# New cost tables and offsets for the planner of a fused attention and gated-MLP kernel

## The chip, the cores and the metric

The kernel runs on one core of one Trainium2 chip. The metric is the device time of one execution in microseconds; a kernel's time is the median over its runs. The engines are TensorE (PE, with its weight loads PEld), VectorE (DVE), ScalarE (ACT), GpSimd (POOL) and SyncE (SP). SP issues all of the kernel's DMAs, on one queue.

## The reference

Four batches of 768 tokens, eight heads of 64 channels. Each query sees the keys less than 16 positions away, and 24 block keys, each the channel-wise maximum over 32 keys; the block values are means over 32 values. One softmax runs over both kinds. The result goes through a gated MLP (512 to 1536 to 512). The MLP's weights come as float64.

```python
k_sum = k.reshape(B, H, nb, block, D).max(axis=3)
v_sum = v.reshape(B, H, nb, block, D).mean(axis=3)
mask_l = np.abs(pos[:, None] - pos[None, :]) < window
scores_s = scale * np.einsum('bhsd,bhnd->bhsn', q, k_sum) + np.log(block)
scores_all = np.concatenate([np.where(mask_l, scores_l, -1e9), scores_s], axis=-1)
a = softmax(scores_all)          # exp, sum + 1e-9, division
x = np.matmul(a, np.concatenate([v, v_sum], axis=2))    # then heads side by side
g = x @ w_gate
out = (g * (1.0 / (1.0 + np.exp(-g))) * (x @ w_val)) @ w_out
```

## The kernel before

**Attention** works on units `(k, u)`: `k` is one of eight half batches of 384 tokens, `u` one of four pairs of heads. For a unit, TensorE makes the scores of six tiles of 64 queries against 96 keys and 24 block keys (step `SC`, line 561). DVE finds the maxima (`max`, or `ttr` from the second batch on), ACT does six `exp` steps with running sums, and `eps`, `rcp` and `nrm` divide. TensorE transposes (`PP`, line 677), ACT or DVE copies out of PSUM (`pt`), and TensorE multiplies by the values (`XO`, line 710). The block keys come from `pool` (line 500) over the whole key rows `kt`, the block values of batches 1 to 3 from `vpool` (line 782) over the rows `vt`. The first batch reads keys straight from `kt`; later ones load overlapping windows `kw` and `vw`.

**The MLP** computes in a float32 form that TensorE passes once. Each operand is split into a high and a low part, and three products are summed (low-high, high-low, high-high). In batch 0 each of twelve slices `j` of the hidden width is multiplied plainly (`u_plain`, line 1014). Meanwhile each weight slice is loaded as raw float64 (`raw_w`, 1 MB) and decoded: `abs` on ACT, `clamp`, `shift`, `sign`, `low` on DVE (lines 896 to 919), then `hi` on ACT and `lo` on DVE or POOL. Four sums of weight blocks (`sumA22` and so on, 128 x 256 elements) follow on POOL or DVE; the sums (`sf`) and part of the split weight (`wa`) are stored to HBM. The output weights (`raw_o`) are decoded likewise. In batches 1 to 3 seven block products take the place of eight (`u_seven`, line 1038); they reload `wa` (`la`) and the sums (`ls`: in batch 1 `sf`, which is split again and stored as `ss`, then `ss`). Weights go through four slots of SBUF, two for each slice. Every three slices the hidden values are multiplied by the output weights (`downs`, line 1108) and added into `part`.

**The order** is set by a planner that runs while the kernel is built. Each piece of work is a `Step` with a cost in microseconds for each engine that may run it, and with the steps it depends on. `run` simulates the engines: it starts on each engine the ready step that is due earliest (`late`), and puts a step that several engines could do on the one that would finish it first. DMA is one engine there, working on one transfer at a time; a transfer costs its bytes over 0.33 MB a us, and its user can start `LAG[DMA]`, 1.9 us, after it. TensorE has two lines whose own order is fixed, the MLP's main line and the attention at its side, which are merged. `NUDGES` is a table of offsets: `name +x` moves a step's due time, `s` sets a slack in TensorE's merging, and `d`, `a` or `p` pins a step to DVE, ACT or POOL. The simulated order is then emitted as the fixed order of each engine's instructions and of SP's DMAs; on the chip each instruction waits for what it needs, and what is queued behind it on its engine waits with it.

**Fillers.** `warm_up` puts dummy matmuls (line 1143) in front of a TensorE step of the first 110 simulated us where the plan has TensorE idle: one for each 0.25 us of the idle time less 0.5, at most ten. Each appears in the trace as two matmuls. Eleven more stand at the very beginning (line 1150).

The helper lines 442 (ACT copy), 444 (DVE or POOL copy), 447 (two-operand arithmetic) and 461 (DMA issue) stand for many steps in the profile; there the tiles' names tell which.

Of the kernel before, what the change touches and what calls it, by code (L numbers as in the profile page):

```python
# [88 lines left out]
def cost(e, kind, n):  # L89

    if kind == "copy":
        return {DVE: 0.12 + 0.0006 * n, ACT: 0.11 + 0.00098 * n, POOL: 0.09 + 0.00108 * n}[e]
    if kind == "evict":
        return {DVE: 0.155 + 0.00104 * n, ACT: 0.11 + 0.00098 * n}[e]
    if kind == "scalar":
        return 0.15 + 0.00052 * n
    return {DVE: 0.155 + 0.00108 * n, POOL: 0.13 + 0.00235 * n}[e]


def on(engines, kind, n):  # L100
    return {e: cost(e, kind, n) for e in engines}

# [84 lines left out]
LAG = {PE: 0.28, DMA: 1.9}  # L187
# [13 lines left out]
kt(0,1) -60.2; id_sb -72.2; vr(1) -12.4; kt(0,0) +8.2; kt(0,2) +20.3; pool(0,2) +97.4; vn(0) +23.7; bias_sb +35.4  # L201
scl1(0,3) -50.5 d; exp2(0,3) -108.4; exp5(0,3) -90; SC(0,0) s0.8; exp0(0,0) -54.7; exp1(0,0) -34.7; exp3(0,0) +137.8
eps(0,0) +172; pt0(0,1) -21.9 a; FV(0) s3.1402; fv(1) -145.6 d; scl0(0,2) -147.8 a; scl1(0,2) +24.3 a
exp1(0,2) -29.2; pt1(0,3) -40.9 a; val2(1) -76.3 p; val1(3) +102.8 p; val2(3) -44 d; xh(3,0) +24.3; PP0(0,0) s2.5
raw_w0 +14.7; low_w0 +106.4; wa0 +51.7; odd2(0) -51 p; val1(0) -42.4 p; odd2(2) -53.7 a; val1(2) -102.9 p
XO(0,2) s0.3; raw_w1 +25.9; max1(1,0) +3.5; eps(1,0) +4.9 d; raw_w2 +6.1; sign_w2 -120.3; sumA11_w2 -94.3 d
sumA12_w2 +63.7 p; vw(1,1) +44.9; max0(1,1) +42.9; scl0(1,1) +5.3; eps(1,1) -27.6 d; mul(1,0) +11.9
values(1,0) -18.1 p; pt1(1,0) +7.8 a; xl(0,1) +43.1; max0(1,2) -57.5; scl0(1,2) +130.9; eps(1,2) +44.3
mul(2,0) -15.7; values(1,1) -41 a; XO(1,1) s0.2; xh(1,1) +34 d; xl(1,1) -53.1; max0(1,3) -109.1; exp2(1,3) +22.1
exp3(1,3) +5.5; exp4(1,3) +47.8; eps(1,3) +121.7 p; raw_o0 +23.5; low_o0 +69.4; lo_o0 +58.3 d; raw_o2 +48.5  # L210
clamp_o2 +42.7; sign_o2 +45.2; raw_w3 +21; sumA11_w3 +28 d; sumA12_w3 +25.7 d; hl(0,3,0) -0.6 p; values(1,2) -20.1 a
xh(2,1) -22.5 d; xl(2,1) -26.5; hh(0,3,1) +12.7 d; sumA12_w4 +42.4; raw_o4 +35.9; hh(0,4,0) -12.1 d; kw(2,0) +115.8
vpool(1,0) +88.1; join(2,0) -32.5 p; kt(1,1) +70.8; pool(1,1) +78.9; ttr0(2,0) -54.6; ttr1(2,0) -49.1; SC(2,1) s1.3
ttr0(2,1) -55.2; ttr1(2,1) -123.6; eps(2,1) +41.2 p; silu(4,1) -103.9; mul(4,1) -59.5; hh(0,4,1) -34 d
hl(0,4,1) +64.3 d; clamp_w5 +65.2; shift_w5 +79.9; lo_w5 -50.4 d; wa5 +68.8; hh(0,5,0) +68.1; PP0(2,0) s3
vs(1,0) -17.4; pt1(2,0) +26.7 d; pt0(2,1) -53.5 a; values(2,0) +106.8; values(2,1) +67.6 p; hh(0,5,1) +6.8
vpool(1,2) +63.1; XO(2,0) s0.6; xf(2,0) +17 d; exp4(2,2) -57.9; exp5(2,2) -28.1; exp1(2,3) -93.2; exp2(2,3) -55.9
exp3(2,3) -123.9; exp4(2,3) +44.1; part(0,1,4) +39.9; part(0,1,5) +61.9; abs_w6 +81.1; shift_w6 +15.1
sumA22_w6 -0.2 p; sumA21_w6 +86.8; silu(6,0) +36.6; hl(0,6,0) -20.6 p; pt0(2,3) +18.3 d; PP1(2,3) s1.6
hl(0,6,1) -27.5 d; shift_w7 +106.2; sign_w7 +34.6; sumA11_w7 +27.6 d; sf7 +9.9; q(3,0) -160.7; kw(3,0) -21.8  # L220
# [32 lines left out]
def order(steps):  # L253
# [13 lines left out]
    for _ in range(3):  # L267
        late = {}
        for s in reversed(steps):
            x = wanted.get(s, 1e9)  # L270
            for o in s.next:
                x = min(x, late[o] - (LAG.get(o_engine(s), 0.12) if s.after is not None else 0))
# [15 lines left out]
def run(steps, line, late):  # L288
# [5 lines left out]
    free = {PE: 0.0, DVE: 0.0, ACT: 0.0, POOL: 0.0, DMA: 0.0}  # L294
# [14 lines left out]
    def close(s):  # L309
        lag = LAG.get(s.engine, 0.12) if s.engine else 0.0  # L310
# [9 lines left out]
    while n:  # L320
        best = None
        for e, waiting in ready.items():
# [13 lines left out]
            else:  # L336
                def start_of(x, s):
                    t = max(free[x], at[s])
                    if x == POOL:
# [27 lines left out]
        if e == POOL or e == DVE and s.port:  # L367
# [12 lines left out]
        if e == POOL or e == DVE and s.port:  # L380
# [10 lines left out]
def body(ctx, tc, qP, kP, vT, vP, wgv, wo, bias, parts, ident, mean, out):  # L391
# [68 lines left out]
    def add_dma(name, nbytes, out, in_, reads, writes):  # L460
        plan.add(name, {DMA: nbytes / 0.33e6}, lambda e: nc.sync.dma_start(out(), in_()), reads, writes)
# [33 lines left out]
    def a_pool_keys(b, u):  # L495
# [8 lines left out]
        plan.add(f"pool({b},{u})", {DVE: 0.95}, do, (kt,), (ks,), port=False)  # L504
# [33 lines left out]
    def a_scores(k, u):  # L538
# [41 lines left out]
        plan.add(f"SC({k},{u})", {PE: (0.85 if direct else 0.64) + 0.55 * biased}, do, [q, *keys] + [parts_sb, id_r] * biased, sc, mode="s")  # L580

    def a_softmax(k, u):
# [818 lines left out]
```

## Time and profile before

| | |
|---|---|
| median of three runs | 687.18 us (686.03 to 687.99) |
| the profiled execution | 690.92 us |
| its span, first to last instruction | 689.1 us |
| busy: PE, PEld, DVE, ACT, POOL | 673.0, 621.2, 515.4, 352.0, 96.8 us |
| granted TensorE clock, mean | 0.999 |
| DMA moved | 149.19 MB, 217 GB/s over the span |

The profiled execution is one execution and has its own time; it lies 3.74 us above the median. Busy time of PE counts the fillers too. A row with `[x <-y]` tells that the engine was idle for x us before it and what ended that. A wait's row names who waited for whom, the total, how many times and the longest. The landing time of a DMA runs from its issue to its last byte's signal, and so includes what was queued before it.

### The profile page before, as it was taken

How to read it: one execution, taken by the hardware profiler on the slowest of the kernel's cores; microseconds unless marked ns; L12 is line 12 of the kernel's file. 1: busy time of each engine (PE TensorE's matmuls, PEld its weight loads, DVE VectorE, ACT ScalarE, POOL GpSimd, SP SyncE). 2: the span in 40 equal slices, each digit the busy share in tenths (PEclk: the TensorE clock that was granted, in tenths of full speed). 3: DMA queues.
4: the chain of work that ended last, by engine and by line, in shares of the span. 5: the costliest groups of instructions: out<-in, count | busy, mean ns of one | idle time of the engine just before them, and what ended most of it. 6: DMA issues, size and time to landing. Idle time of an engine off the chain costs nothing.

```text
span 689.1 us, 13426 instructions
## 1 busy us (share of the span) xinstructions
PE 673.0 (98%) x5156; PEld 621.2 (90%) x5156; DVE 515.4 (75%) x1141; ACT 352.0 (51%) x855; POOL 96.8 (14%) x109
## 2 busy tenths in 40 slices
PE   9899999989999999999999999999999999999997
PEld 8799899889899998889899898989999898989896
DVE  4999999879988795796868875776758762646464
ACT  3889656658675375664534285745435333313130
POOL 0414203213444300010110110100100000000000
PEclk9999999999999999999999999999999999999999
DMA  8899758478758587787857574764615552535222
GB/s 305 299 357 324 255 202 267 163 254 263 246 199 295 204 294 245 233 267 241 289 163 253 201 273 149 231 202 151 235 35 208 193 218 104 214 107 214 107 107 92
DMA packets 69471, 149.19 MB, mean 217 GB/s; under 512 B 22752, under 2 KB 45088, under 8 KB 62496
## 3 DMA queue, kind: packets, MB, share of 16 engines
q1 hardware_dynamic: 69408, 148.35, 62.9%
q8 instruction: 40, 0.66, 0.4%
q14 instruction: 23, 0.19, 0.1%
HBM read 113.73 MB, written 34.60 MB: 215 GB/s over the span
## 4 chain that ended last, share of the span: by engine, by line
PE 75%; DMA 10%; DVE 10%; issue 2%; ACT 2%; POOL 1%; SPq 1%; ACTq 0%; POOLq 0%; DVEq 0%
PE p L1038 32%; PE acc L1108 25%; PE g L1014 5%; DMA s<-ss 4%; PE v L1014 4%; PE xo L710 3%; PE sc L561 2%; PE pp L677 2%; DMA sf<-m_w 2%; DMA kt<-in_kP 1%; DVE m_w L919 1%; DVE m_w L913 1%; DMA vt<-in_vT 1%; POOL m_w L447 1%; DMA wa<-wa 1%
## 5 line engine op out<-in xcount | busy, mean ns | idle before, releaser
L1108 PE MATMUL acc<-o,hh 128*128 128x512 f32 x576 | 179.4, 392 | 0.6 <-DVE o L447 0.6
L1108 PEld LDWEIGHTS acc<-o,hh 128*128 128x128 f32 x576 | 107.1, 188 | 23.2 <-DVE o L447 0.9
L1038 PE MATMUL p<-xh_T,s 128*128 128x384 f32 x432 | 122.8, 339 | 1.8 <-DMA s<-ss 1.3
L1108 PE MATMUL acc<-o,hl 128*128 128x512 f32 x288 | 112.5, 391 | 0.0
L1038 PE MATMUL p<-xh_B,wa 128*128 128x384 f32 x288 | 84.8, 335 | 0.0
L442 ACT COPY s<-p 128x384 f32<-128x384 f32 x64 | 30.8, 481 | 102.8 <-PE p L1038 102.8
L1038 PEld LDWEIGHTS p<-xh_T,s 128*128 128x128 f32 x432 | 79.0, 188 | 4.8 <-DMA s<-ss 3.1
L447 DVE TENSOR_TENSOR part<-acc,part 128x512 f32<-128x512 f32 x72 | 47.9, 688 | 33.2 <-PE acc L1108 33.2
L1038 PE MATMUL p<-xl_T,s 128*128 128x384 f32 x216 | 72.2, 334 | 0.0
L1108 PEld LDWEIGHTS acc<-o,hl 128*128 128x128 f32 x288 | 54.0, 188 | 11.5
L1014 PE MATMUL g<-xh_B,w 128*128 128x384 f32 x192 | 53.9, 341 | 3.2 <-DVE w L447 1.7
L604 ACT ACTIVATE p<-p,nm 128x120 f32<-128x120 f32 x144 | 55.1, 384 | 1.1 <-DVE nm L592 0.6
L447 DVE TENSOR_TENSOR c<-p,u 128x384 f32<-128x384 f32 x72 | 39.8, 554 | 20.4 <-PE p L1038 19.9
L447 DVE TENSOR_TENSOR hl<-a,hh 128x384 fp32r<-128x384 f32 x87 | 51.6, 595 | 3.4 <-ACT hh L442 0.6
L442 ACT CAST hh<-a 128x384 fp32r<-128x384 f32 x52 | 26.6, 515 | 53.0 <-DVE a L447 51.5
L1038 PEld LDWEIGHTS p<-xh_B,wa 128*128 128x128 f32 x288 | 53.0, 188 | 0.1
L1014 PE MATMUL v<-xh_B,w 128*128 128x384 f32 x192 | 52.9, 336 | 0.0
L1038 PE MATMUL p<-xl_B,wa 128*128 128x384 f32 x144 | 48.1, 334 | 0.0
L1038 PE MATMUL p<-xh_B,s 128*128 128x384 f32 x144 | 42.6, 336 | 2.1 <-DVE v L447 2.1
L447 DVE TENSOR_TENSOR a<-c,a 128x384 f32<-128x384 f32 x69 | 39.8, 580 | 4.7 <-ACT a L996 2.1
L1038 PE MATMUL p<-xh_T,wa 128*128 128x384 f32 x144 | 42.4, 335 | 0.0
L1038 PEld LDWEIGHTS p<-xl_T,s 128*128 128x128 f32 x216 | 40.6, 188 | 0.3
(141 smaller groups left out, 1330.6 us busy)
## 6 DMA issues: line engine op xcount, KB each, us to landing
wa<-wa SPq DMA_DIRECT2D x36, 768.0 KB, 4.4
s<-ss SPq DMA_DIRECT2D x24, 1024.0 KB, 7.4
raw_w<-in_wgv SPq DMA_DIRECT2D x12, 1024.0 KB, 6.0
ss<-s SPq DMA_DIRECT2D x12, 1024.0 KB, 5.5
wa<-w SPq DMA_DIRECT2D x12, 768.0 KB, 5.8
vw<-in_vP SPq DMA_DIRECT2D x28, 288.0 KB, 4.9
kw<-in_kP SPq DMA_DIRECT2D x24, 288.0 KB, 5.5
kt<-in_kP SPq DMA_DIRECT2D x16, 400.0 KB, 6.8
```

The lines of the kernel that those rows point to most:

```text
L442: nc.scalar.copy(out, in_)
L447: vector[e].tensor_tensor(out=out, in0=a, in1=b, op=op)
L561: nc.tensor.matmul(make(sc[h])[s * QT : (s + 1) * QT, c * KC + at : c * KC + at + x.shape[-1]], make(q)[hs, qs], x, start=not biased or c ...
L604: nc.scalar.activation(out=make(p)[:, i, :], in_=make(p)[:, i, :], func=AF.Exp, scale=-1.0, bias=make(nm)[:, i : i + 1], accum_out=make(sm ...
L677: nc.tensor.transpose(make(pp)[:KC, c * P : (c + 1) * P], make(p)[:, g * NT // 2 + c, :], make(id_sb))
L710: nc.tensor.matmul(ps[hs, qs], v, make(pt)[:, h, qs], start=True, stop=True)
L913: lambda e: nc.vector.scalar_tensor_tensor(out=bits(), in0=high(), scalar=-0x40000000, in1=bits(), op0=ALU.bitwise_and, op1=ALU.bitwise_or ...
L919: lambda e: nc.vector.scalar_tensor_tensor(out=bits(), in0=low(), scalar=29, in1=bits(), op0=ALU.logical_shift_right, op1=ALU.bitwise_or), ...
L1014: nc.tensor.matmul(t[:, :TOK], a, x, start=u == 0 and n == 0, stop=u == NP - 1 and n == 2)
L1038: nc.tensor.matmul(t[:, :TOK], a, x, start=first and kk == 0 and n == 0, stop=kk == 1 and n == 2, skip_group_check=not first,)
L1108: nc.tensor.matmul(ps, a, w, start=j == js[0] and m == 0, stop=j == js[-1] and m == 2)
```

## The change

The arithmetic stays as it is. The costs in the planner are replaced; they grow for some steps and shrink for others. A new kind `strided` stands for the copies of the first batch's values. A new function costs a transfer by the size of its rows. `FIRST` says from when on each engine is free in the plan. The cap on fillers goes from 10 to 30. The table of offsets is replaced as a whole.

```diff
 def cost(e, kind, n):
     if kind == "copy":
-        return {DVE: 0.12 + 0.0006 * n, ACT: 0.11 + 0.00098 * n, POOL: 0.09 + 0.00108 * n}[e]
+        return {DVE: 0.12 + 0.00055 * n, ACT: 0.16 + 0.00083 * n, POOL: 0.09 + 0.00108 * n}[e]
+    if kind == "strided":
+        return {DVE: 0.165 + 0.001 * n, ACT: 0.14 + 0.00096 * n, POOL: 0.09 + 0.00108 * n}[e]
     if kind == "evict":
-        return {DVE: 0.155 + 0.00104 * n, ACT: 0.11 + 0.00098 * n}[e]
+        return {DVE: 0.13 + 0.00104 * n, ACT: 0.115 + 0.00084 * n}[e]
     if kind == "scalar":
-        return 0.15 + 0.00052 * n
-    return {DVE: 0.155 + 0.00108 * n, POOL: 0.13 + 0.00235 * n}[e]
+        return 0.11 + 0.00054 * n
+    return {DVE: 0.13 + 0.00104 * n, POOL: 0.13 + 0.00235 * n}[e]

+ROW = {"kt": 3200, "kw": 384, "vn": 1024, "vw": 512, "q": 1536, "la": 6144, "wa": 6144, "raw": 8192, "ss": 8192, "sf": 4096, "ls": 8192}
+
+def moved(name, nbytes):
+    kind = next((k for k in ROW if name.startswith(k)), None)
+    row = ROW.get(kind, 2048)
+    took = nbytes / row * (0.009 + row * 0.0000366) / 16
+    return took * {"ls": 1.45 if nbytes > 1e6 else 1.8, "vw": 1.4, "kw": 1.2}.get(kind, 1.0)

-LAG = {PE: 0.28, DMA: 1.9}
+LAG = {PE: 0.23, DMA: 2.35}
+FIRST = {PE: 5.4, DVE: 0.0, ACT: 0.0, POOL: 0.0, DMA: 0.4}
...
-    free = {PE: 0.0, DVE: 0.0, ACT: 0.0, POOL: 0.0, DMA: 0.0}
+    free = dict(FIRST)
...
-        lag = LAG.get(s.engine, 0.12) if s.engine else 0.0
+        lag = LAG.get(s.engine, 0.07) if s.engine else 0.0
...
-        plan.add(name, {DMA: nbytes / 0.33e6}, ...)
+        plan.add(name, {DMA: moved(name, nbytes)}, ...)
...
-        plan.add(f"SC({k},{u})", {PE: (0.85 if direct else 0.64) + 0.55 * biased}, ...)
+        plan.add(f"SC({k},{u})", {PE: (1.2 if direct else 0.6) + 0.63 * biased}, ...)
...
-                plan.add(f"ttr{g}({k},{u})", {DVE: 1.1}, ...)
+                plan.add(f"ttr{g}({k},{u})", {DVE: 0.67}, ...)
...
-                    plan.add(f"exp{i}({k},{u})", {ACT: 0.62}, ...)
+                    plan.add(f"exp{i}({k},{u})", {ACT: 0.44}, ...)
...
-            spare[0] = min(10, max(0, int((s.idle - 0.5) / 0.25)))
+            spare[0] = min(30, max(0, int((s.idle - 0.5) / 0.25)))
```

Of the offsets, those that pin the weight sums of the first four slices and a `nrm` (the rest of the table, some 200 entries before and after, is left out):

```diff
-sumA11_w2 -94.3 d
-sumA12_w2 +63.7 p
-sumA11_w3 +28 d; sumA12_w3 +25.7 d
+sumA12_w0 -23.8 d
+sumA22_w1 -15.2 d
+sumA22_w2 +21.5 d; sumA11_w2 -52.9 p
+sumA12_w2 +50.1 p
+nrm(1,2) +13.1 p
+sumA22_w3 -71 p; sumA11_w3 +107.8 p
```

Further costs move by a few hundredths (`pool`, `vpool`, `max`, `scl`, `rcp`, `nrm`, `PP`, `FV`, the products and the down-projection), `eps` on POOL goes from 0.18 to 0.24. Steps of POOL and of DVE that share the memory port are treated alike in the simulation (`s.port`), which names no step that was treated otherwise before.

More of the change, by code (lines that the diff above doesn't have):

```diff
@@ L216 @@
[L216 to L220, printed above, removed]
@@ L271, in order @@
             for o in s.next:
-                x = min(x, late[o] - (LAG.get(o_engine(s), 0.12) if s.after is not None else 0))
+                x = min(x, late[o] - (LAG.get(o_engine(s), 0.07) if s.after is not None else 0))
             late[s] = x - min(s.engines.values(), default=0)
@@ L338, in start_of @@
                     t = max(free[x], at[s])
-                    if x == POOL:
+                    if x == POOL and s.port:
                         t = max(t, held[DVE])
@@ L366, in run @@
         (start, _, s), e = best
-        if e == POOL or e == DVE and s.port:
+        if e in (POOL, DVE) and s.port:
             start = max(start, held[POOL if e == DVE else DVE])
@@ L379, in run @@
         s.idle = start - free[e]
-        if e == POOL or e == DVE and s.port:
+        if e in (POOL, DVE) and s.port:
             held[e] = s.end - HOLD
@@ L460, in add_dma @@
     def add_dma(name, nbytes, out, in_, reads, writes):
-        plan.add(name, {DMA: nbytes / 0.33e6}, lambda e: nc.sync.dma_start(out(), in_()), reads, writes)
+        plan.add(name, {DMA: moved(name, nbytes)}, lambda e: nc.sync.dma_start(out(), in_()), reads, writes)
     def aside(f):
@@ L502, in do @@
             )
-        plan.add(f"pool({b},{u})", {DVE: 0.95}, do, (kt,), (ks,), port=False)
+        plan.add(f"pool({b},{u})", {DVE: 0.92}, do, (kt,), (ks,), port=False)
     def a_queries(k, u):
@@ L578, in do @@
                         )
-        plan.add(f"SC({k},{u})", {PE: (0.85 if direct else 0.64) + 0.55 * biased}, do, [q, *keys] + [parts_sb, id_r] * biased, sc, mode="s")
+        plan.add(f"SC({k},{u})", {PE: (1.2 if direct else 0.6) + 0.63 * biased}, do, [q, *keys] + [parts_sb, id_r] * biased, sc, mode="s")
     def a_softmax(k, u):
@@ L641, in a_softmax @@
                 if on_bank(k, u):
-                    plan.add(f"exp{i}({k},{u})", {ACT: 0.62}, lambda e, i=i: bank_exp(i), (sc[g], (nm, g)), ((p, g), (sm, g)), table="exp")
+                    plan.add(f"exp{i}({k},{u})", {ACT: 0.44}, lambda e, i=i: bank_exp(i), (sc[g], (nm, g)), ((p, g), (sm, g)), table="exp")
                 else:
-                    plan.add(f"exp{i}({k},{u})", {ACT: 0.62}, lambda e, i=i: one_exp(i), ((nm, g),), ((p, g), (sm, g)), table="exp")
+                    plan.add(f"exp{i}({k},{u})", {ACT: 0.44}, lambda e, i=i: one_exp(i), ((nm, g),), ((p, g), (sm, g)), table="exp")
         def guard(e):
@@ L650, in guard @@
                 vector[e].tensor_scalar(out=make(sm), in0=make(sm), scalar1=1e-9, scalar2=None, op0=ALU.add)
-        plan.add(f"eps({k},{u})", {DVE: 0.18, ACT: 0.22, POOL: 0.18}, guard, (), (sm,))
-        plan.add(f"rcp({k},{u})", {DVE: 0.18}, lambda e: nc.vector.reciprocal(out=make(ri), in_=make(sm)), (sm,), (ri,), port=False)
+        plan.add(f"eps({k},{u})", {DVE: 0.14, ACT: 0.18, POOL: 0.24}, guard, (), (sm,))
+        plan.add(f"rcp({k},{u})", {DVE: 0.16}, lambda e: nc.vector.reciprocal(out=make(ri), in_=make(sm)), (sm,), (ri,), port=False)
         def scale(e):
@@ L659, in scale @@
             )
-        plan.add(f"nrm({k},{u})", {POOL: 1.4, DVE: 0.9}, scale, (ri,), (p,))
+        plan.add(f"nrm({k},{u})", {POOL: 1.4, DVE: 0.88}, scale, (ri,), (p,))
     @aside
@@ L784, in do @@
             )
-        plan.add(f"vpool({b},{u})", {DVE: 0.95}, do, (vt,), (vr,), port=False)
+        plan.add(f"vpool({b},{u})", {DVE: 0.92}, do, (vt,), (vr,), port=False)
     def a_keep_values(b, u, pp):
@@ L1014, in do @@
                         nc.tensor.matmul(t[:, :TOK], a, x, start=u == 0 and n == 0, stop=u == NP - 1 and n == 2)
-            plan.add(f"{which}({j},{hf})", {PE: 12 * 0.175}, do, [w] + sum(ops, []), (acc,))
+            plan.add(f"{which}({j},{hf})", {PE: 12 * 0.1737}, do, [w] + sum(ops, []), (acc,))
         a = buf("x", f"a{hf}", [P, TOK], f"a_0_{j}_{hf}")
@@ L1041, in do @@
                     )
-        plan.add(f"{name}({b},{j})", {PE: 6 * 0.1745}, do, [src] + sum(ops, []), (acc,))
+        plan.add(f"{name}({b},{j})", {PE: 6 * 0.1737}, do, [src] + sum(ops, []), (acc,))
     def u_seven(b, j):
@@ L1112, in piece @@
             reads = sum(([*HH[b, j, hf], O[j][0]] for j in todo), [])
[L1113 removed]
+            plan.add(f"D{n}({b},{g},{t})", {PE: 0.227 * 3 * len(todo)}, do, reads, (acc,))
         def finish():
```

80 lines of the change are left out of this document (43 added, 37 removed).

## The prediction

> **What bounds the kernel now.** I read the page's head first, then a table of the engines' busy time by stage (stages cut where the first dense stretch of TensorE begins, 82.2 us, and where its waits stop, 345 us), then TensorE's waits by releaser, and last the order of time around the waits.
>
> ```profile
> span 689.1 us, 13426 instructions
> PE 673.0 (98%) x5156; PEld 621.2 (90%) x5156; DVE 515.4 (75%) x1141; ACT 352.0 (51%) x855; POOL 96.8 (14%) x109
> ```
> ```profile
> 0.00:20.00 20.00, 18.90 (x280) 17.90 (x282) 9.58 (x20) 7.74 (x31) 3.40 (x10) 1.00 0.84 292
> 20.00:40.00 20.00, 17.39 (x295) 15.93 (x290) 19.77 (x35) 17.23 (x52) 8.11 (x9) 1.00 0.90 331
> 40.00:56.50 16.50, 15.63 (x214) 14.90 (x212) 16.50 (x32) 15.57 (x35) 0.00 (x0) 1.00 0.96 348
> 56.50:82.20 25.70, 24.89 (x240) 22.09 (x241) 25.26 (x41) 20.08 (x46) 11.53 (x11) 1.00 0.87 294
> 82.20:210.00 127.80, 125.43 (x965) 116.25 (x965) 113.21 (x250) 84.67 (x188) 35.56 (x39) 1.00 0.68 226
> 210.00:345.00 135.00, 132.35 (x1025) 121.30 (x1024) 107.52 (x269) 74.41 (x190) 23.46 (x26) 1.00 0.77 261
> 345.00:555.00 210.00, 209.98 (x1486) 194.63 (x1485) 153.41 (x370) 101.79 (x257) 14.76 (x17) 1.00 0.57 191
> 555.00:689.00 134.00, 128.43 (x667) 118.22 (x665) 70.19 (x130) 30.46 (x61) 0.00 (x0) 0.99 0.40 145
> ```
>
> The columns are the stretch, its length, then busy time of PE, PEld, DVE, ACT and POOL, the granted clock, the DMA share and GB/s. TensorE is the bound, and from 345 to 555 us nothing is left to win: 209.98 of 210. Between 82.2 and 345 it is idle 2.37 + 2.65 = 5.02 us, and that is all that an order could win there. Before 82.2 the picture is another: DVE is full (19.77 of 20, 16.50 of 16.50, 25.26 of 25.70), ACT and DMA nearly, and TensorE's busy time is in part not work. The next row is line 1143 alone, the filler matmuls of `warm_up`:
>
> ```profile
> 0.00:82.20 82.20, 16.60 (x130) 15.30 (x130) 1.00 0.89 313
> ```
>
> So of the first 82.2 us TensorE spends 16.60 on fillers and is idle for another 82.20 - 18.90 - 17.39 - 15.63 - 24.89 = 5.39. The waits by releaser:
>
> ```profile
> PE p L1038 <- DVE v L447: 2.1, 2, 1.4
> PE g L1014 <- DVE w L447: 1.7, 2, 0.9
> PE pp L677 <- ACT w L442: 1.6, 1, 1.6
> PE p L1038 <- DMA s<-ss: 1.3, 3, 0.5
> PE g L1014 <- DVE part L447: 1.0, 1, 1.0
> PE g L1014 <- ACT a L996: 0.6, 1, 0.6
> ```
>
> In the middle part TensorE waits for DVE and ACT steps. DVE was not short of time there (107.52 of 135 busy); it stood at a DMA in its own fixed order, and the step that TensorE wanted was queued behind:
>
> ```profile
> 285.12 0.70 DVE L444 CAST s<-s 128x1024 fp32r<-128x1024 f32 x1 [2.85 <-DMA s<-sf]
> 285.73 0.55 DVE L447 TENSOR_TENSOR v<-p,s 128x384 f32<-128x384 f32 x1
> 318.08 0.95 DVE L500 TENSOR_REDUCE ks<-kt 128x24 f32<-128x768 f32 x1 [2.20 <-DMA kt<-in_kP]
> 143.21 0.95 DVE L782 TENSOR_REDUCE vr<-vt 128x24 f32<-128x768 f32 x1 [3.06 <-DMA vt<-in_vT]
> ```
>
> Each time the engine's order holds a step that needs a transfer at a place where the planner thought it landed. The planner's costs for transfers, which the change rewrites, decide where that place is.
>
> **The change part by part.** No instruction of the computation is added or removed; the number of filler matmuls, the order on each engine, the order of the DMA queue and the engine of some steps change. Of TensorE's main line the order is fixed (`line[0]` runs in the order of the program), so only the attention steps move within it.
>
> *Costs of transfers.* The landing times on the page, issue to landing:
>
> ```profile
> kt<-in_kP SPq DMA_DIRECT2D x16, 400.0 KB, 6.8
> s<-sf SPq DMA_DIRECT2D x12, 512.0 KB, 5.7
> vt<-in_vT SPq DMA_DIRECT2D x12, 384.0 KB, 6.6
> s<-ss SPq DMA_DIRECT2D x24, 1024.0 KB, 7.4
> ```
>
> Before, kt costs 409,600 / 0.33e6 = 1.24 plus a lag of 1.9 = 3.14 us; after, 128 rows x (0.009 + 3200 x 0.0000366) / 16 = 1.01 plus 2.35 = 3.36. For s<-sf: 1.59 + 1.9 = 3.49 before, 64 x 0.3088 / 16 x 1.8 + 2.35 = 4.57 after. For vt 3.09 before and 3.36 after, for s<-ss 5.08 and 5.93. All still lie under the medians, which hold the queueing behind other transfers that the planner adds by its one serial DMA. So the plan moves towards the trace by 0.2 to 1.1 us a transfer, where the stalls of DVE were 2.2 to 3.1. The costs alone would not clear them; offsets chosen over varied DMA times may, by putting such steps later. I take half of the 5.02 us: **-2.5**. Ends: -5.0 (all gone), and +3.0, which is one new stall of DVE as long as the three rows above, with TensorE behind it. I take the half as DVE has 20% of slack in that part, so a step that waits for a transfer can go behind the one that TensorE wants at no price.
>
> *The last stages.* Three waits for s<-ss, 1.3 us in all, lie after 555 us. Each copy can only start once the slot two weights back is free (four slots, two a weight), and the product that covers it is fixed. **0**, bounds -1.3 to +1.0 (one more of three waits, twice as long).
>
> *Costs of engines.* An `exp` was put at 0.62 and is put at 0.44; direct scores at 1.40 and now 1.83. The trace, first and fourth of consecutive exps, and the first matmuls of a scores step and of the one after it:
>
> ```profile
> 11.44 0.35 ACT L628 ACTIVATE p<-sc,nm 128x120 f32<-128x120 f32 x1
> 12.45 0.37 ACT L628 ACTIVATE p<-sc,nm 128x120 f32<-128x120 f32 x1
> 41.34 0.42 PE L561 MATMUL sc<-kt,q 64*64 64x96 f32 x8
> 43.27 0.42 PE L1014 MATMUL g<-xh_B,w 128*128 128x384 f32 x1
> ```
>
> An exp takes (12.45 - 11.44) / 3 = 0.34, where the planner (which lets steps overlap by 0.06) counted 0.56 and will count 0.38; the scores take 1.93. Per softmax of six exps the old plan had ACT late by 1.3 us, over eight softmaxes 10.6, and TensorE early by 8 x 0.53 = 4.2. In the opening stage its order was therefore made for another machine. What it cost shows where TensorE waited for the third weight:
>
> ```profile
> 53.14 2.48 PE L1143 MATMUL g<-warm 128*128 128x128 f32 x20
> 56.49 0.44 PE L1014 MATMUL g<-xh_B,w 128*128 128x384 f32 x1 [0.87 <-DVE w L447]
> 42.16 1.22 DVE L913 SCALAR_TENSOR_TENSOR m_o<-raw_o,m_o 128x1024 int32<-128x1024 int32 x1
> 49.20 1.22 DVE L919 SCALAR_TENSOR_TENSOR m_o<-raw_o,m_o 128x1024 int32<-128x1024 int32 x1
> ```
>
> 2.48 of fillers and 0.87 of idle time, 3.35 us, while DVE had put two large steps of an output weight in front, which no product before the fourth up-projection reads. But DVE is full up to 82 us: work put behind the third weight comes due later, and only what isn't needed before 82 (pooling and the decoding of the next output weight) is a true gain. I take a third of the 3.35: **-1.1**, ends -3.35 and 0, and +2.4 on the other side, if the new order twice lets a softmax that TensorE needs wait behind a decode step of 1.22.
>
> *DVE to POOL.* Of the weight sums before 82 us, three pins name DVE and one POOL in the old offsets (weights 0 to 3), three DVE and four POOL in the new, and one `nrm` more is pinned to POOL. POOL stands still from 40 to 56.5 us (0.00 above).
>
> ```profile
> L447 DVE TENSOR_TENSOR m_w<-m_w 128x256 f32<-128x256 f32 x9 | 3.7, 414 | 0.0
> L656 DVE TENSOR_TENSOR p<-p,ri 128x720 f32<-128x720 f32 x6 | 5.7, 956 | 0.1
> 53.38 0.66 DVE L906 TENSOR_SCALAR m_w<-m_w 128x1024 int32<-128x1024 int32 x1
> 66.49 1.21 DVE L906 TENSOR_SCALAR m_o<-m_o 128x1024 int32<-128x1024 int32 x1
> 65.76 1.39 POOL L656 TENSOR_TENSOR p<-p,ri 128x720 f32<-128x720 f32 x1
> ```
>
> If all of these were on DVE, it is relieved of 3 x 0.41 + 0.96 = 2.2 us. But beside POOL's `nrm` the same shift took 1.21 in place of 0.66, so a `nrm` moved saves 0.96 - 0.55 = 0.41, and with a like toll of half on the sums 3 x 0.2: **-1.0**, ends -2.2 and 0.
>
> The Trainium skill (GPSIMD Engine Reference, section "8. Key points") says that GpSimd shares its SBUF interfaces with VectorE and that they contend where DVE works in a 2-port mode or with two SBUF inputs; by that rule taken at its full price the move gives DVE nothing and the sum would be 1.0 us higher, while by the quiet durations it would be 1.2 lower. The two rows at 53.38 and 66.49 agree with the rule, and the measured toll is what I took.
>
> *Longer fillers.* At most 30 instead of 10 in a row, the number still by the planned idle time less 0.5 us. The clock is 1.00 in every stretch up to 555 us, so there is no clock to win. Where the plan holds, they end before the operands do: **0**; ends 0 and +2.9 a time (third rival). Before the first scores the plan now counts TensorE's idle time from 5.4 us and not from 0, so a run of fillers goes (2.40 us, the first row). DVE, which takes up the scores, waits for a transfer later anyway (second row): 0, ends -0.5 and 0.
>
> ```profile
> 5.21 2.40 PE L1143 MATMUL sc<-warm 128*128 128x128 f32 x20
> 13.80 0.95 DVE L500 TENSOR_REDUCE ks<-kt 128x24 f32<-128x768 f32 x1 [1.96 <-DMA kt<-in_kP]
> ```
>
> **Sum**: -2.5 - 1.1 - 1.0 = -4.6. The profiled execution took 690.92 us (span 689.1 and 1.8 around it), which becomes 686.3. It lies 3.74 over the median of the runs, 687.18, so the forecast for the median is 687.18 - 4.6 = **682.6**.
>
> **Rivals.** *Nothing to be told.* DVE in the opening stage is a queue that is never empty, so its order does not change when the last of it ends; and kt's new cost of 3.36 is still half of 6.8, so new stalls replace old ones. For it: DVE's 16.50 of 16.50 and the small steps of the DMA costs. Against it: DVE does work there that isn't due. Only 0.5 is won: 686.7. This is also the case in which the change does not do what it says.
>
> *Much more.* All 5.0 us in the middle, the 3.35 at the third weight and 1.2 of DVE's relief: 687.18 - 9.6 = 677.6. For it: 16.60 + 5.39 us of TensorE's opening are not work. Against it: the full DVE.
>
> *Slower: fillers that can't be given up.* A run of fillers has a fixed length. With ten the rest of a long idle stretch absorbs lateness; with thirty (three times the 2.40 of ten, 7.2) the stretch is filled to 0.5 us of its planned end, and a TensorE that comes late stays late, with SC, softmax and DVE behind it. A kt planned at 3.36 and landing at 6.8 is 3.4 late, 2.9 of it beyond the half microsecond. It decides where the planned idle exceeds 0.5 + 10 x 0.25 = 3.0 us (a run of exactly 20 matmuls is such a place, and g at 53.14 is one) and TensorE arrives over 0.5 late. Two such, with half of the middle won: +5.8 - 2.5 = +3.3, 690.5. Against it: fillers fall away where the plan has less idle time, and the longest wait for operands before is 1.6.
>
> **How the numbers follow.** Forecast (682.6, own range 680 to 685.5) 0.48; nothing 0.22; much more 0.12; slower 0.18. The three runs shown lie within 0.3%, so I call under 0.3% (2.06 us) the same: faster is under 685.1, slower over 689.2. From the forecast 0.45 of 0.48 is faster, from "nothing" 0.03 of 0.22, "much more" wholly: 0.60; same 0.22; slower 0.18. The range must reach "much more" below (677) and most of the slower case above (689.8); about 0.07 is left out below and 0.1 above.
>
> **What would show it.** Right: the row from 210 to 345 us has PE idle for 1.5 or less in place of 2.65, the stalls of DVE at kt and s<-sf go or no PE wait follows them; from 0 to the first dense weight fillers and idle together fall by about 2 us; sums on POOL rise above seven before 82 us with DVE's shift steps at 1.2 more often; three waits for s<-ss stay at the end. Wrong: PE idle after 82 us as before or larger, with new releasers (the first rival), or a line 1143 well over 16.60 with no wait behind it and scores that start late (the third).

## The result and the profile after

| | before | after |
|---|---|---|
| median of nine runs each | 686.83 us (684.41 to 688.96) | 682.92 us (680.62 to 686.02) |
| ratio, with its 95% interval | | 0.9948 [0.9923, 0.9973] |
| the profiled execution, and its span | 690.92, 689.1 us | 682.90, 681.1 us |

The change makes the kernel about 0.5% faster: 0.52% of 686.83 is 3.6 us, and the interval runs from 1.9 to 5.3. The two profiled executions lie further apart (8.0 us) than the medians (3.9), since that of before was a long one. Medians count every execution, ratios leave out single far longer ones (1884.24 us once for the changed kernel, 1861.95 once for before, 694.14 once for the first hybrid below). Line numbers after are those of before plus 15 (1014 becomes 1029, 1038 becomes 1053, 1108 becomes 1123, 1143 becomes 1158). First the page's head and the table by stage of the changed kernel, with the columns as before:

```profile
span 681.1 us, 13314 instructions
PE 668.3 (98%) x5096; PEld 617.0 (91%) x5096; DVE 523.4 (77%) x1156; ACT 346.7 (51%) x849; POOL 91.2 (13%) x98
```
```profile
0.00:20.00 20.00, 16.98 (x250) 14.97 (x252) 10.44 (x27) 8.84 (x34) 2.50 (x9) 0.91 0.92 325
20.00:40.00 20.00, 18.38 (x292) 16.54 (x287) 19.54 (x34) 16.91 (x49) 4.14 (x5) 1.00 1.04 335
40.00:56.50 16.50, 15.71 (x204) 14.74 (x203) 16.50 (x28) 16.41 (x38) 0.24 (x1) 1.00 1.06 358
56.50:82.20 25.70, 24.56 (x240) 21.97 (x239) 25.61 (x40) 17.50 (x47) 9.89 (x9) 1.00 0.79 264
82.20:210.00 127.80, 125.54 (x1001) 116.68 (x1000) 123.26 (x265) 84.94 (x189) 36.76 (x35) 0.99 0.72 245
210.00:345.00 135.00, 135.00 (x998) 123.91 (x997) 108.47 (x269) 72.02 (x189) 30.35 (x29) 1.00 0.75 252
```

From 210 to 345 us TensorE no longer stands still (135.00 of 135, before 132.35). From 82.2 to 210 it is idle for 2.26 us, nearly as before (2.37), but in one piece, the first of these waits of the whole execution:

```profile
PE acc L1123 <- ACT hh L457: 2.3, 1, 2.3
PE sc L576 <- DMA q<-in_qP: 2.0, 2, 1.7
PE xo L725 <- DVE pt L459: 0.9, 1, 0.9
PE pp L692 <- DVE p L671: 0.7, 1, 0.7
PE g L1029 <- DVE w L462: 0.5, 1, 0.5
PE p L1053 <- DMA s<-ss: 0.2, 1, 0.2
```

The waits `p <- v` (2.1), `g <- w` (1.7), `pp <- w` (1.6), `g <- part` (1.0) and `g <- a` (0.6) of before are gone or small; new are 2.3 us for a cast of hidden values and, in the opening, 2.0 for queries. The row of fillers alone, up to 82.2 us:

```profile
0.00:82.20 82.20, 9.63 (x70) 8.43 (x70) 0.98 0.94 315
```

9.63 us of fillers in place of 16.60, though the cap rose: the plan, which sets their number by the idle time that it expects, now holds 35 of them (70 matmuls) where it held 65. Only one row of them is longer than ten (13 planned, 26 matmuls, in front of a `PP`).

What DVE waited for from 82.2 to 345 us, before and then after (engine, step and line; releaser; us in total, times, longest):

```profile
DVE vr L782 <- DMA vt<-in_vT: 8.9, 2, 5.8
DVE ks L500 <- DMA kt<-in_kP: 4.9, 4, 2.2
DVE s L444 <- DMA s<-sf: 4.7, 3, 2.8
```
```profile
DVE s L459 <- DMA s<-sf: 3.6, 3, 2.4
DVE ks L515 <- DMA kt<-in_kP: 0.9, 1, 0.9
```

18.5 us in which DVE's queue stood at one of these transfers have become 4.5. DVE did not become busy for all of that time: after the change it stands for TensorE's scores instead, mostly in one stall.

```profile
DVE p L607 <- PE sc L576: 8.4, 2, 7.5
```

### The profile page after: what moved, and what is told of

Read it like the earlier page. It is cut to its first block, busy times and chain, and to the rows that moved or that the text cites. A ratio compares the mean times of both kernels' runs of the same rounds, so it can differ in the third digit from the quotient of the medians.

```text
span 681.1 us, 13314 instructions
## 1 busy us (share of the span) xinstructions
PE 668.3 (98%) x5096; PEld 617.0 (91%) x5096; DVE 523.4 (77%) x1156; ACT 346.7 (51%) x849; POOL 91.2 (13%) x98
## 4 chain that ended last, share of the span: by engine, by line
PE 85%; DVE 8%; DMA 4%; issue 1%; ACT 1%; SPq 0%; ACTq 0%
PE p L1053 38%; PE acc L1123 28%; PE g L1029 5%; PE v L1029 5%; PE sc L576 3%; PE xo L725 3%; PE pp L692 2%; DMA raw_w<-in_wgv 1%; DMA s<-ss 1%; DMA q<-in_qP 1%; DVE m_w L928 1%; DVE m_w L934 1%; DMA kt<-in_kP 1%; DVE m_w L462 1%; DVE nm L629 1%
## 5 line engine op out<-in xcount | busy, mean ns | idle before, releaser
L457 ACT COPY s<-p 128x384 f32<-128x384 f32 x58 | 27.7, 480 | 96.8 <-PE p L1053 96.8
L607 DVE CUSTOM_DVE_ANT_0 p<-sc,bias_sb 128x120 f32<-128x120 f32 x144 | 30.3, 276 | 15.6 <-PE sc L576 15.3
```

Of the source, the lines that this page charges most:

```text
L457: nc.scalar.copy(out, in_)
L607: nc.vector.tensor_tensor_reduce(out=make(p)[:, i, :], in0=make(sc[g])[:, c * KC : (c + 1) * KC], in1=make(bias_sb)[:, 0 if n == 0 else 2 ...
```

## The experiments

How far an execution had come is read from the start of the n-th matmul of the products' lines (the up-projection and `downs`, 2,952 matmuls in all, counted from 0; attention and fillers are not counted). Each entry is the difference in us from the profile of before, whose own starts stand in the first row. Attention steps sit at other places in other orders, so a single entry can be off by one such step; the columns that matter are those where the sign stays.

| profile | n=48 | 144 | 240 | 576 | 1344 | 2928 |
|---|---|---|---|---|---|---|
| before, start | 56.49 | 85.71 | 103.85 | 185.45 | 354.80 | 679.28 |
| before_again | +1.27 | +1.26 | +1.26 | -0.51 | -3.56 | -5.26 |
| after | -1.46 | -2.70 | +1.34 | -1.46 | -5.65 | -7.58 |
| after_again | -1.76 | -3.00 | -1.51 | -4.31 | -8.34 | -9.19 |
| h1_new_opening | +0.38 | -0.37 | +2.36 | +1.42 | +0.25 | -1.07 |
| h2_old_opening | +1.43 | +0.99 | +1.30 | -1.45 | -5.91 | -6.35 |
| e_swap | -1.61 | -2.82 | -0.03 | -2.25 | -6.18 | -7.00 |
| e_swap2 | -1.09 | -2.32 | -1.78 | -2.61 | -6.71 | -7.59 |
| e_swap3 | +0.36 | -0.86 | -0.83 | -1.53 | -5.76 | -7.28 |
| n_new | +0.49 | +2.39 | +2.60 | +2.07 | +0.12 | -0.72 |
| n_mixed | -1.20 | +6.20 | +8.04 | +4.60 | +5.49 | +4.67 |
| n_old | +6.17 | +13.01 | +13.01 | +11.05 | +12.37 | +9.63 |

**The same two kernels once more.** No edit; a second profile of each.

> The kernel before, unchanged, profiled once more. Theory: the two profiles on record differ by 8.0 us of span where the medians differ by some 3.6, and the last 1.9 us of the 8.0 (from 555 us on, where both kernels have the same order of instructions and of transfers) are a matter of one execution: here the waits for s<-ss after 555 us come out differently from 1.3 us, anywhere between 0 and 2, and the span between 683 and 688. Rival: the tail belongs to the order; then the waits are 1.3 us again and the span 689. The waits in the middle (DVE v, DVE part, DVE w, in all about 5 us between 82 and 345 us) should return by both, since they hang on the order.

> The kernel after, unchanged. Theory: the wait of TensorE for a hidden value behind the decode of the fifth weight (2.3 us near 92 us) belongs to the order and returns, between 1.5 and 3.5 us, and with it a stretch at half the granted clock in most executions. From 100 to 550 us TensorE waits for nothing. Time 682 to 684. Rival: that wait is one late transfer of one execution; then it is gone here, and the time of most executions already has it left out.

Before: 685.67 us. Its middle part, the same program as the one in the prediction:

```profile
82.20:210.00 127.80, 127.50 (x983) 118.95 (x984) 116.71 (x254) 86.02 (x191) 37.49 (x39) 1.00 0.69 230
210.00:345.00 135.00, 134.00 (x1032) 123.02 (x1031) 108.88 (x274) 75.64 (x196) 23.76 (x25) 1.00 0.79 264
```

0.30 + 1.00 = 1.30 us of idle time in place of the 5.02 on which the prediction rests; the expectation that the waits in the middle would return failed. One order, fixed in the program, gave both figures. DVE's stalls differ less between these two executions than TensorE's idle time:

```profile
DVE vr L782 <- DMA vt<-in_vT: 7.2, 2, 5.9
DVE ks L500 <- DMA kt<-in_kP: 4.1, 4, 1.8
DVE s L444 <- DMA s<-sf: 2.3, 3, 1.5
```

13.6 us against 18.5. The changed kernel again: 684.81 us, ratio 0.9945 [0.9923, 0.9967]; DVE's stalls there were 2.3 us (4.5 in the first profile), TensorE's idle time from 82.2 to 345 us 0.92 + 0.13 (2.26 + 0). Here the two fall alike, so that stalls are the steadier measure holds for the old order alone. The 2.3 us for the cast `hh` did not return; in their place stands

```profile
PE acc L1123 <- DVE hl L462: 0.9, 2, 0.7
```

The waits for `s<-ss` at the end were 1.3 us in three, where the first profile has 0.2 in one; before, they were 1.3 in three and 0.2 in one. So those waits, too, change from one execution to the next of the same program.

**Which half of the order gives the gain.** Two kernels take the step order, engines and fillers of one plan up to the first product of the second token half, `g(0,1)` (about 80 us), and the rest from the other plan. The arithmetic is the same.

```diff
-    for s in order(plan.steps):
-        if s.engine == PE and s.start < 110.0:
-            spare[0] = min(30, max(0, int((s.idle - 0.5) / 0.25)))
+    for row in ORDER:              # written down from the two plans
+        name, e, fill = row.split("|")
+        s = by_name[name]
+        s.engine = e or None
+        spare[0] = int(fill)
```

> The new order up to the first product of the second token half (79.5 us in the profile after), with its engines and fillers, and for all steps left the order of before. Theory (the opening and the middle win apart from each other): the opening wins the 2.7 us by which that product starts earlier in the two profiles, and the old waits of the middle come back: 684.2, between 683 and 685.5. Rival 1 (DVE's queue is never empty until 210 us, so what the opening wins is waited for again behind it): 686.5 to 687.5. Rival 2 (all of the gain is in the opening): 683.

> The order of before up to the first product of the second token half (82.2 us in the profile before), with its engines and fillers, and for all steps left the new order. Theory: the middle wins 3.0 us by itself (from the two profiles between that product and 345 us: 5.65 less 2.70), so 683.9, between 682.5 and 685.5; its profile has no wait of TensorE between 130 and 345 us, and the wait near 92 us for a hidden value behind the decode of the fifth weight is there. Rival 1 (the rest only wins with its opening): 686.5 or more. Rival 2 (all in the rest): 683 or less.

New opening with the old rest: 688.63 us, ratio 1.0007 [0.9982, 1.0031]. Old opening with the new rest: 683.98 us, 0.9943 [0.9921, 0.9964], as much as the whole change. The middle part of each, first with the old rest, then with the new:

```profile
82.20:210.00 127.80, 125.09 (x959) 115.10 (x959) 113.78 (x250) 84.87 (x188) 35.45 (x39) 1.00 0.68 228
210.00:345.00 135.00, 132.38 (x1026) 121.65 (x1026) 106.67 (x268) 74.44 (x188) 21.93 (x25) 1.00 0.77 257
```
```profile
82.20:210.00 127.80, 127.78 (x1026) 119.34 (x1023) 125.94 (x268) 85.12 (x190) 36.91 (x35) 1.00 0.73 246
210.00:345.00 135.00, 135.00 (x1000) 124.17 (x999) 107.75 (x269) 72.11 (x189) 28.97 (x29) 1.00 0.76 250
```

5.33 us of idle time against 0.02. The gain sits in the order from the second token half on. The opening's own head start is real in the two profiles of after (n=144: 2.7 and 3.0 us), yet by the medians it doesn't reach the end. In the one profile of the new opening with the old rest it was 0.4 us at n=144; there the granted clock of the first 20 us was 0.83, in the two of after 0.91 and 1.00.

**Where the head start goes.** Between n=144 and n=240 the row of after goes from -2.70 to +1.34. That stretch as the chain of waits of the changed kernel has it (start, length, what), and then the two engines' lines in time:

```profile
84.97 8.05 DMA raw_w<-in_wgv
...
94.42 0.51 ACT hh L457
```
```profile
93.40 1.12 ACT L911 ACTIVATE m_w<-raw_w 128x1024 f32<-128x1024 f32 x1 [5.15 <-DMA raw_w<-in_wgv]
94.42 0.50 ACT L457 CAST hh<-a 128x384 fp32r<-128x384 f32 x1
```
```profile
94.97 1.22 PE L1123 MATMUL acc<-o,hh 128*128 128x512 f32 x2 [2.26 <-ACT hh L457]
95.99 0.63 PE L1123 MATMUL acc<-o,hl 128*128 128x512 f32 x1
...
98.65 0.62 PE L1123 MATMUL acc<-o,hh 128*128 128x512 f32 x2
99.10 0.39 PE L1123 MATMUL acc<-o,hl 128*128 128x512 f32 x1
```

In this profile ACT stands for 5.15 us at the fifth weight's `abs`; the cast `hh` that the down-projection wants is queued behind it, and TensorE waits 2.26 us. After that wait the same matmuls run at half speed for a while (two in 1.02 us, 94.97 to 95.99, against 0.45 later, 98.65 to 99.10). Before, ACT had the same two steps in the same order; below them the issue of the weight on SP's queue, and TensorE's down-projection in the chain of waits:

```profile
92.27 1.15 ACT L896 ACTIVATE m_w<-raw_w 128x1024 f32<-128x1024 f32 x1 [2.42 <-DMA raw_w<-in_wgv]
93.33 0.50 ACT L442 CAST hh<-a 128x384 fp32r<-128x384 f32 x1
```
```profile
86.42 8.65 SPq L461 DMA_DIRECT2D raw_w<-in_wgv  x3
```
```profile
94.71 6.16 PE acc L1108 x27
```

There `hh` was ready at 93.8, and TensorE's down-projection began only at 94.71, so nobody saw the wait. An opening that is 2.7 us earlier ran into a weight that came 1.1 us later: issued at 84.97 instead of 86.42, 1.45 us sooner, but with 8.05 us to its landing, so its `abs` started at 93.40 instead of 92.27.

The second profile of after shows the other case. There the weight was issued at 84.91 and its `abs` started at 90.20; the waits there came to 0.9 us. Against h2_old_opening, which has the same order from the second half on, that execution was 4.0 us ahead at n=144 and still 2.8 at n=2928, where the first one had 3.7 and kept 1.2. In the profile of h1_new_opening `abs` started at 94.10, and 2.7 us were lost between n=144 and 240. So whether the head start lasts goes with the landing of this one weight; three executions show it side by side, the next edits try it.

They move the steps that TensorE wants out from behind the weight. First on both engines, roughly:

```diff
 # the fifth weight's abs, clamp, shift, sign and the sixth's abs
-ACT: abs w4 | hh(0,1,1) | hi o6 | silu(2,1) | hh(0,2,1) | abs w5 | abs o8
+ACT: hh(0,1,1) | hi o6 | silu(2,1) | hh(0,2,1) | abs o8 | abs w4 | abs w5
-DVE: clamp w4 | hl(0,1,1) | shift w4 | mul(2,1) | sign w4 | hl(0,2,1)
+DVE: hl(0,1,1) | mul(2,1) | hl(0,2,1) | clamp w4 | shift w4 | sign w4
```

> The order after, with one edit: the first four decode steps of the fifth weight (abs on ACT, clamp, shift and sign on DVE, and the sixth weight's abs, which must follow) go behind the hidden values of the first three slices of the second token half (hh and hl of slice 2), so nothing that the down-projection near 92 us needs is queued behind the landing of that weight. Theory (what the opening won is paid back at that one place): the wait of 0.9 to 2.3 us goes, and the stretch at half clock behind it that cost another 1.8 where it came; TensorE stays busy from 92 to 130 us; 1.5 to 4 us faster than after, ratio to before 0.989 to 0.992. Rival (DVE's queue is the bound up to 210 us): the wait only moves, to the fifth weight's first product, where TensorE now waits for the decode that came later, and the time is that of after, ratio 0.994 to 0.995.

683.93 us, 0.9949 [0.993, 0.9968]. The wait moved by one product:

```profile
102.66 0.44 PE L1029 MATMUL v<-xh_B,w 128*128 128x384 f32 x1 [2.50 <-DVE part L459]
```

The copy `part(0,0,3)`, which frees the PSUM tile of that product, now stood on DVE behind the decode; and `abs o8`, left ahead of `abs w4`, held the weight on ACT. The wait only moved and the time is that of after, as the rival had it; but part of the edit stood in its own way, so it doesn't decide. Before a cleaner one, two trials of the fillers, since the first half-speed stretch of the changed kernel followed a wait of 1.70 us for the queries of the second unit of scores:

```diff
-SC(0,3): 3 fillers
+SC(0,3): 10 fillers        # e_both: and the edit above
```

> The order after, with ten fillers instead of three ahead of the second unit's scores (as many as before the change). Theory: TensorE's wait of 1.6 to 1.7 us for q near 10 us is what lets the granted clock fall to half for 3.4 us at 11.6 to 12.9 us in two of three profiles of this opening; with fillers up to 10.9 us there is no such stretch. Since DVE is full, this is worth little: 0.3 us (the two profiles of after, with and without that stretch, stand 0.3 apart at 85 us), up to 1 us; ratio 0.993 to 0.995. Rival (fillers cost time where the operands come before they end): up to 0.5 us slower than after.

> Both edits together. Theory: the sum, 1.5 to 5 us faster than after, ratio to before 0.988 to 0.992. Rival: as after, 0.994 to 0.995.

685.6 us, 0.9958 [0.9938, 0.9978], and 685.59 us, 0.9974 [0.9953, 0.9996]: nothing won. The half-speed stretch in the opening was absent in these profiles at that place, but others came at 95.65 us, and at 23.68 and 105.6.

```diff
+ACT: silu(1,1) | hh(0,1,1) | hi o6 | silu(2,1) | hh(0,2,1) | abs w4 | abs w5 | part(0,0,4) | part(0,0,5) | hi w4 | silu(3,1) | abs o8
+DVE: low o6 | hl(0,1,1) | mul(2,1) | hl(0,2,1) | clamp w4 | shift w4 | sign w4 | part(0,0,3) | low w4 | clamp w5 | shift w5 | lo w4
```

> The changed kernel with the order of two engines edited between 88 and 100 us, on both sides of the fifth weight's landing: DVE does the two steps hl of the second and third slice and the product before them ahead of the weight's clamp, shift and sign, then the copy of part(0,0,3), then the rest; ACT does both hh casts ahead of the weight's abs, and the output weight's abs after both copies of part. TensorE's order and all arithmetic stay. Theory (the decode of the fifth weight stands too early in the new order, for its slot only comes free with the product before it and it lands late; what is queued behind it on DVE and ACT is what TensorE wants): TensorE is idle for under 1 us between 82.2 and 110 us, no wait there has DVE or ACT as releaser for over 1 us, and the head start of the opening (2.4 to 3 us) stays: ratio to the kernel before 0.989 to 0.992. Rival (the weight is late whatever stands around it, and the wait only moves to the next product that needs it): 0.994 to 0.996, with a wait of 2 us or more at the fourth or fifth slice's product.

682.21 us, 0.9913 [0.989, 0.9935]. TensorE's waits from 82.2 to 345 us, and the stretch in question:

```profile
PE g L1029 <- DVE w L462: 0.7, 1, 0.7
PE g L1029 <- ACT a L1011: 0.6, 1, 0.6
```
```profile
82.20:110.00 27.80, 26.95 (x183) 24.53 (x182) 24.84 (x34) 15.85 (x20) 4.00 (x2) 1.00 0.64 217
```

0.85 us idle and the full clock, where the first profile of after has 27.80 - 25.54 = 2.26 at a clock of 0.94 (the second, in which the weight landed early, 0.92 at 1.00). At n=240 it is 3.1 us ahead of the first, 0.3 of the second; of the 3.1, 2 are lost by n=288 to 336 in two waits of 0.7, and in work that stood elsewhere. Against the first, 1.06 are left at n=1344, and the last of it goes at the end, where this profile has 1.0 us of waits for `s<-ss` and after 0.2. So the single profiles show the wait gone, not a faster execution; for the time only the medians speak.

```diff
-DVE: ... part(0,0,3) | low w4 | clamp w5 | shift w5 | lo w4
+DVE: ... low w4 | clamp w5 | lo w4 | shift w5
-ACT: ... abs w5 | part(0,0,4) | part(0,0,5)
+ACT: ... abs w5 | part(0,0,3) | part(0,0,4) | part(0,0,5)
```

> The order of the run e_swap2 with two more edits: the copy of part(0,0,3) goes from DVE to ACT, ahead of the other two copies of part, and DVE's shift of the sixth weight stands behind the fifth weight's lo. That takes 0.68 + 0.69 us from DVE between the fifth weight's landing and its lo, for which the fifth slice's first product waited 0.73 us at 104 us; ACT stands idle there until the cast hi of that weight. Theory (the fifth weight's decode is all that binds TensorE between 90 and 110 us once the steps for TensorE stand ahead of it): that wait goes, no wait over 0.4 us between 82.2 and 110 us, and the median lies 0.5 to 1 us under that run's: ratio to the kernel before 0.988 to 0.992. Rival (that run's time was luck of landings, and the time of the new order is what the changed kernel has): ratio 0.994 to 0.996.

683.3 us, 0.9916 [0.9887, 0.9945] (beside a before of 688.98 in that comparison). The wait for `w` went, as expected, and no wait is left between 82.2 and 345 us but one:

```profile
PE g L1029 <- ACT a L1011: 1.4, 1, 1.4
```

The time is that of e_swap2: no further 0.5 us can be told. So with the steps for TensorE ahead of the weight, two kernels gave 0.9913 and 0.9916, the changed kernel 0.9948 and 0.9945. The means differ by 0.0032; taking the four intervals as independent, the difference's own interval is about 0.0026 to either side. The four were measured in different comparisons, and e_swap2 and e_swap3 are the best of five tries. I take it as likely, not as settled, that this version beats the changed kernel, by about 2 us; against before the gain of 0.9% is clear.

**Costs and offsets apart.** Three kernels run the planner with an empty table of offsets: with all new costs, with the new engine costs but the old cost of transfers, and with all old costs.

```diff
-NUDGES = """ kt(0,1) -33.6; q(0,1) -20.3; ... """
+NUDGES = ""
-LAG = {PE: 0.23, DMA: 2.35}                   # n_mixed alone, with the next edit
+LAG = {PE: 0.23, DMA: 1.9}
-        plan.add(name, {DMA: moved(name, nbytes)}, ...)
+        plan.add(name, {DMA: nbytes / 0.33e6}, ...)
```

> The new costs with no offsets at all (the table emptied, all else as after). Theory, as the prediction had it (the costs alone do not clear the stalls, the offsets do): slower than before, 690 to 700, with waits of TensorE in the middle stage of more than 5 us. Rival (the costs carry the gain and the offsets little): 683 to 686, and less than 2 us of waits between 82 and 345 us.

> The changed kernel with an empty table of offsets, and with the old cost of a transfer (bytes over 0.33 MB a us, 1.9 us until its user can start) beside the new costs of the engines. Theory (in the plain plan the costs of transfers decide where DVE stands at a transfer): slower than with all new costs and no offsets, ratio to the kernel before 1.004 to 1.008, TensorE idle for over 4 us between 82.2 and 345 us with waits for steps of DVE and transfers. Rival (the costs of transfers do not matter at these sizes, since a landing is late by more than either cost says): ratio 0.998 to 1.002, and idle time there of 2 to 3 us as with all new costs (2.4).

> The kernel before with its own costs and an empty table of offsets: the plain plan of the old costs. With the new costs and no offsets the ratio was 1.000. Theory (the costs are worth nothing by themselves, only a table of offsets fitted to its own costs gives time): the same as with the new costs and no offsets, ratio 0.997 to 1.003, so the old offsets were worth nothing and only the new ones are. Rival (better costs are worth what the offsets are): slower than the kernel before by as much as the new offsets give, ratio 1.004 to 1.010, as old offsets repaired what the old costs had wrong; the idle time of TensorE from 82.2 to 345 us is then over 5 us.

| costs, no offsets | median | ratio to before |
|---|---|---|
| new | 688.0 us | 1.0004 [0.9987, 1.0021] |
| new engines, old transfers | 694.33 us | 1.0094 [1.0068, 1.012] |
| old | 702.07 us | 1.0213 [1.0182, 1.0244] |

The theory that costs are worth nothing by themselves falls. The new costs alone do what the old costs did with 200 offsets: without offsets they are worth 2.1%. Replaced in this order (the other was not run), 0.9% of it is the cost of transfers and 1.2% the rest, that is the costs of the engines with `FIRST`, the other lags and the cap on fillers. The offsets gave 2.1% on the old costs and give 0.5% on the new. In the middle TensorE's idle time without offsets is 2.43 us with all new costs, 4.75 with the old transfers, 5.03 with all old:

```profile
82.20:345.00 262.80, 260.37 (x2021) 239.75 (x2022) 233.91 (x557) 156.67 (x372) 26.87 (x31) 1.00 0.73 243
82.20:345.00 262.80, 258.05 (x2023) 238.92 (x2024) 229.68 (x533) 155.57 (x359) 31.34 (x32) 1.00 0.71 239
82.20:345.00 262.80, 257.77 (x1925) 238.05 (x1925) 225.72 (x512) 158.49 (x363) 39.92 (x47) 0.99 0.71 234
```

Taken alone this looks like what was expected of the costs of transfers, though two executions of one program lay 3.7 us apart in the same figure. The table of starts says otherwise: n_mixed is behind n_new by 3.8 us at n=144 and by 5.4 at n=240, and by the same 5.4 at the end. What the old costs of transfers lose, they lose before about 110 us, and nothing in the rest of the middle. Of the old costs together, too, most is lost before n=144 (13.0 there, 9.6 at the end); TensorE's largest wait in that profile is for a softmax, three times (its line 645 is the `PP` of 677):

```profile
PE pp L645 <- DVE p L624: 6.4, 3, 3.3
```

## Why the prediction was right, and where it was not

The forecast of 682.6 us met 682.92, but the terms share it out wrongly: of the 4.6 us, 3.6 came (1.9 to 5.3), with one term too small and two that were worth nothing. That they cancelled so nearly is luck.

*The middle, -2.5.* Right in its place and too small; its mechanism is shown in part. The place is shown by the second hybrid: with the old opening kept, the new rest gives 0.57% of 687.54, which is 3.9 us (2.5 to 5.4). DVE's stalls at `kt`, `vt` and `s<-sf` fell from 18.5 and 13.6 us in two profiles to 4.5 and 2.3. That these stalls make up the 3.9 was not shown by an edit of a single one, and a small sum of them is not by itself a fast order: n_old, 2.1% slower than before, has 5.5 + 2.8 + 1.9 = 10.2. The step "The costs alone would not clear them" failed: with new costs and no offsets the same stalls are 2.5 + 1.4 + 1.2 = 5.1. Nor was it the costs of transfers that cleared most of them, as the prediction argued: with the old ones beside the new costs of engines they are 6.3. Which of the new costs and offsets gives the gain of the middle stays open. The size rested on 5.02 us of idle time in one profile; a second one of the same kernel had 1.30.

*The opening, -1.1, and DVE to POOL, -1.0.* Together 2.1; at n=144 2.7 and 3.0 were measured, and at the end nothing that can be told: the new opening alone is 1.0007, from 1.2 us faster to 2.1 slower. The step that failed is that the gain at 82 us was carried to the end with no look at what is late next. The fifth weight was, in the executions where it lands late, and e_swap2 and e_swap3 make it likely that this is where the head start goes: the row of ACT at 92.27 with its 2.42 us of waiting stood in the profile of before, with `hh` behind it and 0.9 us from its end to TensorE's need. The first rival said that the opening wins nothing; its result holds for the opening, its reason does not, since DVE's full queue did let TensorE start 2.7 us earlier.

The move to POOL was wrong even in its sign. Sums of weights up to `g(0,1)` after (first DVE, then POOL; us in total, mean ns), while of the `nrm` two were on POOL and six on DVE, as before:

```profile
L462 DVE TENSOR_TENSOR m_w<-m_w 128x256 f32<-128x256 f32 x12 | 5.1, 445 | 0.0
L462 POOL TENSOR_TENSOR m_w<-m_w 128x256 f32<-128x256 f32 x4 | 3.2, 797 | 22.2 <-DVE w L462 16.6 <-DVE m_w L462 5.6
```

Twelve sums on DVE and four on POOL, where before had nine and seven: 5.1 us of DVE's time instead of 3.7. I read the pins in the table as if the other sums stayed where they were; the planner places those that aren't pinned by its costs. The toll on shifts, and with it the rule that the prediction cites from the Trainium skill, was therefore not put to the test by this change.

*Longer fillers, 0.* Right: fewer fillers, one run above ten, no stretch where TensorE came late behind them. The third rival's condition did not occur. The first scores start at 6.38 instead of 7.54 us, 1.2 earlier, but the first product at 37.24 instead of 36.99: of the up to 0.5 us that the prediction allowed for it nothing came.

*The last stages, 0.* Right within the bounds: the waits for `s<-ss` are 1.3, 0.2 (before) and 0.2, 1.3 (after), and change between executions more than between the kernels.

*What would show it.* The row from 210 to 345 us was to be idle for 1.5 or less and is 0.00; but the second profile of before, with 1.00, would have passed the same test. Fillers and idle time before 82.2 us fell from 16.60 + 5.39 to 9.63 + 6.57, by 5.8 in place of 2; in the second profile, without the stretch of half clock at 12.8 us (below), they are 9.61 + 7.59, 4.8 less. Of that, 3.0 is the head start at n=144; which other work of TensorE makes up the rest was not taken apart. The sums on POOL were to rise above seven and fell to four, which told that the third term was wrong.

## What to carry to other kernels

A head start is worth only what the next late operand leaves of it: before an earlier stage is booked as gain, find the first transfer behind it that may land late, and what stands in the fixed order behind the instruction that waits for it. In a planned order, measure the costs anew before searching offsets: here the new costs alone did the work of some 200 offsets. And take a second profile before a term is sized by idle time at transfers, or a place is named by one: here the idle time of one program was 5.02 and 1.30 us.

## What the runs showed of the hardware

TensorE's granted clock fell to half for some 3.4 us at a time, after waits as short as 1.6 to 2.3 us, at places that differ from one execution to the next of one program. In the first profile of after, the two stretches, each behind a wait (1.70 us at 10.93 for queries, 2.26 us at 94.97 for `hh`), the column before the last two being the clock:

```profile
12.80:16.30 3.50, 3.50 (x35) 2.18 (x36) 2.31 (x7) 2.28 (x11) 0.74 (x2) 0.51 1.08 392
94.80:98.20 3.40, 3.23 (x8) 2.45 (x9) 3.39 (x5) 2.77 (x5) 2.26 (x1) 0.50 0.43 181
```

Half the clock for 3.4 us is worth 1.7 us of TensorE's work. The second profile of after had a wait of 0.7 at the later place and no such stretch there; the second of before had one at 32.77 us behind a wait of 1.60; the first had the same wait (1.61) and no such stretch. The same waits don't always bring it, and what decides it these runs don't tell. In e_swap3, behind a wait of 2.5 us for queries, it lasted longer, and the first product came 1.69 us later than in e_swap2, which had the short stretch at the same place:

```profile
12.00:16.00 4.00, 4.00 (x42) 3.54 (x37) 3.08 (x7) 2.10 (x13) 0.72 (x2) 0.50 1.11 381
16.00:20.00 4.00, 4.00 (x71) 3.09 (x67) 1.38 (x5) 2.37 (x10) 2.04 (x4) 0.65 0.99 403
```

The Trainium skill (TensorE: Matmul & The Clock Gate, section "Part 1: The HAM clock gate (the 'warmup' mystery)") gives a free-running window of about 3.4 us after which the clock is switched; the length of the two stretches above, 3.5 and 3.4 us, agrees with it. Its section "HAM oscillation — how this bites in real kernels" asks for no idle gap of TensorE over about 3.4 us; here waits of 1.6 to 2.3 us were followed by the half clock, so at this kernel's waits that bound doesn't protect.
